# Soft-capped attention into a slot mixture: scores issued right behind tanh, side work in fixed slots, loads per tensor, filler matmuls

## The chip, the cores and the metric

The kernel runs on one NeuronCore of a Trainium2 chip. The core has engines with a queue each that work in order: TensorE (PE in the profile; its weight loads are PEld), VectorE (DVE), ScalarE (ACT), GpSimd (POOL) and SyncE (SP), which here only issues DMAs. TensorE writes to PSUM, eight banks of 2 KB per partition; the other data lie in SBUF. The metric is the device time of one execution in microseconds, the median of several runs. The profile comes from one further execution.

## The reference

Attention over 8 batches x 12 heads, 448 positions, head size 64, with a soft cap on the scores, and behind it a soft mixture of 8 experts with 4 slots each:

```python
scores = scale * q @ k.T                      # per batch and head, scale = 1/8
scores = cap * np.tanh(scores / cap)          # cap = 30
attn = softmax(scores)                        # rows
x = (attn @ v) -> (3584, 768)                 # heads side by side
logits = x @ phi                              # 32 slots
d = softmax(logits, axis=0)                   # over all 3584 rows
slot_input = d.T @ x                          # (8 experts, 4 slots, 768)
slot_out[e] = relu(slot_input[e] @ w1[e]) @ w2[e]     # 768 -> 1024 -> 768
c = softmax(logits, axis=1)                   # over the slots
out = c @ slot_out
```

The attention is where the exponentials are: 8 x 12 x 448 x 448 values go through tanh and then through exp.

## The kernel before, in words

**Tiles.** Four heads of one batch form a quad (24 quads, index Q), two heads a pair (48 pairs). A quad's q, k and v are loaded as f32 (`load`, line 126), 448 KB each, cast to bf16 (`cast`, line 135, on DVE; `vcast`, line 152, on POOL, into block-diagonal tiles `vbd` with a column of ones for the row sums), and q and k are transposed on PE, seven tiles each, with a copy back by DVE (`transp`, line 141). `load` allocates all three raw tiles and issues their three DMAs on SP in the order q, k, v. Each raw tile has one buffer, so a load waits until the cast of the quad before has read it.

**Chunks.** The scores of a pair are seven tiles of 128 keys (two heads of 64) x 448 queries. Four such tiles make a chunk; there are 84 chunks, and seven of them cover two quads. For chunk j: `qk_chunk(j)` (line 166) is eight matmuls into the one PSUM tile `sc` (four banks, one buffer), `tanh_chunk(j)` (line 178) reads it on ACT into `ex`, `exp_chunk(j)` (line 183) works on `ex` in place, and `pv_tile` (line 186), four matmuls per tile, accumulates attention times v and the row sums in `pv`. A pair's seven tiles accumulate in the same two banks, so every seventh tile is a pair's last: there DVE computes reciprocals and scales the result into `xq` (lines 205 and 206), which frees the banks for the next pair. Such a pair's turn falls inside a chunk in three chunks of seven.

**Side work.** Per pair `x_transp` (line 214) transposes `xq`; per quad `logits` (line 223); per batch, that is every three quads, `e_exp` (a small exponential on ACT), `slot_sums` in three parts, `e_transp`, and per two batches `e_sums`. The transposes, the logits and the slot sums share two PSUM buffers (pool `psT`). The expert weights are loaded by POOL's DMA queue, 40 loads spread over the loop: `w1b` (8 tiles), the first 28 blocks of `w2b` into SBUF, the other 36 converted to bf16 in DRAM (`w2d`).

**Order.** The order of each engine's queue is written out by hand; nothing is reordered. The dictionary `aux` maps a chunk number to its side work. One round of the loop (line 333) issues: tanh of j, all 16 matmuls of pv of chunk j-1, all side work of j, the scores of j+1, the exponential of j. On PE the scores of j+1 therefore stand behind everything else of the round. Before the loop come the loads, the clearing of `vbd` on POOL, casts, transposes and `qk_chunk(0)`.

**After the loop.** The last chunk's pv, then the remaining transposes, logits, e_exp and slot sums; then `w2d` is loaded back into SBUF (line 358, on SP, as the attention's SBUF comes free); `layer1` (line 369; PSUM tile `hp`, two buffers), `h_transp`, `layer2` (line 397), and the output stage (from line 425): 28 tiles, each two matmuls, a scaling by ACT or DVE, and a DMA of 384 KB.

Of the kernel before, what the change touches and what calls it, by code (L numbers as in the profile page):

```python
# [8 lines left out]
F32 = mybir.dt.float32  # L9
BF16 = mybir.dt.bfloat16  # L10
# [4 lines left out]
P = 128  # L15
HP = 64
NT = 7
DH = 64
S = 448
CH = 4  # L20
# [7 lines left out]
def kernel(  # L28
# [55 lines left out]
    w1b = [wts.tile([P, NJ, F], BF16, name=f"w1b{e}", tag="w1", bufs=E) for e in range(E)]  # L84
# [13 lines left out]
    wjobs = []  # L98
    for e in range(E):
        for jh in range(NJ // 2):  # L100
            wjobs.append((w1b[e][:, 2 * jh:2 * jh + 2, :],
                          w1r[:, e, 2 * jh:2 * jh + 2, :]))
    for n0 in range(0, R2, 4):
        wjobs.append((w2b[:, n0:n0 + 4, :], w2_src(n0, 4)))
# [3 lines left out]
    for n0 in range(R2, len(blocks), 4):  # L108
        t = dram.tile([P, 4, D], BF16, name=f"w2d{n0}")
        wjobs.append((t, w2_src(n0, 4)))  # L110
        w2d.append(t)
# [14 lines left out]
    def load(Q):  # L126
        b, hq = divmod(Q, NQB)
        for nm, src in (("q", q), ("k", k), ("v", v)):
            t = ld.tile([P, 2, S], F32, name=nm + "raw", tag=nm + "raw")
            sp.dma_start(out=t, in_=bass.AP(  # L130
                tensor=src.tensor, offset=(b * H + 4 * hq) * S * DH,
                ap=[[NT * DH, P], [2 * S * DH, 2], [1, NT * DH]]))
            raws[nm, Q] = t

    def cast(nm, Q):
        t = cst.tile([P, NT, P], BF16, name=nm + "bf", tag=nm + "bf")
        dve.tensor_copy(t.rearrange("p c (h d) -> p h c d", h=2),  # L137
                        raws.pop((nm, Q)).rearrange("p h (c d) -> p h c d", d=DH))
        casts[nm, Q] = t

# [11 lines left out]
    def vcast(Q):  # L152
        raw = raws.pop(("v", Q)).rearrange("p h (c d) -> p h c d", d=DH)
        t = vbds[Q % 2]
        pool.tensor_copy(t[0:HP, :, :, 0:DH], raw[0:HP])  # L155
        pool.tensor_copy(t[HP:P, :, :, DH + 1:VW - 1], raw[HP:P])  # L156

    def init_vbd():
        for t in vbds:
            pool.memset(t, 0.0)  # L160
            pool.memset(t[0:HP, :, :, DH:DH + 1], 1.0)
            pool.memset(t[HP:P, :, :, VW - 1:VW], 1.0)
# [20 lines left out]
    def exp_chunk(j):  # L183
        act.activation(exs[j], exs[j], ACT.Exp, scale=cap)  # L184
# [98 lines left out]

    aux = {}

    def at(j, f, *a):
        aux.setdefault(max(j, 0), []).append((f, a))

    def first_chunk(Q):
        return Q * 2 * NT // CH  # L290

    for Q in range(1, NQ):
        j0 = first_chunk(Q)
        at(j0 - 4, cast, "k", Q)
        at(j0 - 4, cast, "q", Q)
        at(j0 - 3, transp, "k", Q)
        at(j0 - 3, vcast, Q)
        if Q + 1 < NQ:
            at(j0 - 3, load, Q + 1)
        at(j0 - 2, transp, "q", Q)  # L300
    for pr in range(NPAIR):
        jc = (pr * NT + NT - 1) // CH + 1
        Q, h = divmod(pr, 2)
        b, hq = divmod(Q, NQB)
        at(jc + 1, x_transp, pr)
        if h == 1:
            at(jc + 2, logits, Q)
            if hq == NQB - 1:
                at(jc + 3, e_exp, b)
                for part in range(3):  # L310
                    at(jc + 4 + part, slot_sums, b, part, 3)
                if b < B - 1:
                    at(jc + 6, e_transp, b)
                if b % 2 and b < B - 1:
                    at(jc + 7, e_sums, b // 2)
    nw = len(wjobs)
    for n, job in enumerate(wjobs):
        j = 2 + n * (NCH - 8) // nw
        at(j, lambda o, i: pool.dma_start(out=o, in_=i), *job)  # L319


    load(0)
    pool.dma_start(out=phib, in_=moe_phi.rearrange("(jt ji) s -> ji jt s", ji=P))
    init_vbd()
    dve.memset(hpad, 0.0)
    cast("q", 0)
    cast("k", 0)
    vcast(0)
    load(1)
    transp("q", 0)  # L330
    transp("k", 0)
    qk_chunk(0)
    for j in range(NCH):
        tanh_chunk(j)
        if j > 0:
            for t in range((j - 1) * CH, j * CH):
                pv_tile(t)
        for f, a in aux.pop(j, []):
            f(*a)
        if j + 1 < NCH:  # L340
            qk_chunk(j + 1)
        exp_chunk(j)
    for t in range((NCH - 1) * CH, NCH * CH):
        pv_tile(t)
    for j in sorted(aux):
        for f, a in aux[j]:
            f(*a)
# [130 lines left out]
```

## Time and profile before

| | us |
|---|---|
| median of 3 runs | 374.16 (371.19 to 374.2) |
| the profiled execution | 371.95 |
| its span, first to last instruction | 369.8 |
| ACT busy in the span | 294.8 |
| PE busy in the span | 277.5 |
| DVE busy in the span | 159.5 |
| mean granted TensorE clock | 0.881 of full |

Times in the rows of the trace count from the span's start. A row of the timeline has start, duration, engine, line, operation, tiles (out<-in), shapes and count; in brackets stand the idle time of the engine before it and what ended it. A row of the waits has the waiting engine and line, whom it waited for, the total in us, how often, and the longest. In the page's profile by slices (40 equal ones) each digit is a tenth. Matmuls are pipelined, so a group of n takes less than n times one; durations of groups overlap a little with their neighbours.

### The profile page before, as it was taken

Reading aid. Unit: us, or ns where it says so; the run is one execution under the profiler, and the core shown is the slowest. Engines: PE = TensorE matmul, PEld = TensorE weight load, DVE = VectorE, ACT = ScalarE, POOL = GpSimd, SP = SyncE. Lnnn points to the kernel's source line nnn. Section 1 sums busy time; section 2 is a strip of 40 time slices with the busy share of each in tenths; the row PEclk is TensorE's granted clock in tenths of the full one; section 3 lists DMA queues with packets and bytes.
Section 4 is the critical chain, followed back from the end, with each engine's and each line's share of the span. In section 5 each row is a group of like instructions: output and inputs, shape, how many; then the busy total and the mean of one; then the engine's idle time right before and its main releaser. Section 6 shows DMA issues by size and latency. Waiting matters only on the chain.

```text
span 369.8 us, 7691 instructions
## 1 busy us (share of the span) xinstructions
PE 277.5 (75%) x3316; PEld 185.5 (50%) x3316; DVE 159.5 (43%) x403; ACT 294.8 (80%) x194; POOL 83.3 (23%) x113
## 2 busy tenths in 40 slices
PE   2887888779777697888778697777687976697580
PEld 1455655547555465555555464555454654444220
DVE  5234435444454444454364444443643432314552
ACT  1789989997998979999889989999899899013441
POOL 8401331223033214312330340233213200000000
PEclk9999869996899979988898969999989698589956
DMA  8795769873976788698749899899898920682997
GB/s 209 227 230 114 200 177 220 188 197 116 222 203 185 180 163 219 160 248 173 195 138 224 210 249 245 187 281 240 200 190 229 209 86 2 235 364 108 396 398 293
DMA packets 40705, 76.83 MB, mean 208 GB/s; under 512 B 3168, under 2 KB 29792, under 8 KB 40672
## 3 DMA queue, kind: packets, MB, share of 16 engines
q1 hardware_dynamic: 24912, 51.13, 40.4%
q0 software_dynamic: 15760, 25.22, 37.6%
q8 instruction: 26, 0.43, 0.5%
q14 instruction: 7, 0.06, 0.0%
HBM read 90.54 MB, written 18.09 MB: 294 GB/s over the span
## 4 chain that ended last, share of the span: by engine, by line
PE 38%; ACT 37%; DVE 14%; DMA 5%; issue 3%; SPq 0%; DVEq 0%; ACTq 0%
ACT ex L184 19%; ACT ex L181 17%; PE pv L196 14%; PE sc L175 12%; DVE xq L206 7%; DMA out_dram<-ob 3%; PE kps L145 2%; DVE rec L205 2%; DMA kraw<-in_k_dram 2%; PE hp L375 2%; PE xps L218 2%; PE so_ps L401 1%; PE op L433 1%; PE lps L228 1%; DVE ob L437 1%
## 5 line engine op out<-in xcount | busy, mean ns | idle before, releaser
L181 ACT ACTIVATE ex<-sc 128x1792 bf16<-128x1792 f32 x84 | 139.3, 1658 | 31.3 <-PE sc L175 31.1
L196 PE MATMUL pv<-vbd,ex 128*128 128x130 bf16 x1344 | 119.5, 242 | 52.6 <-DVE xq L206 25.4
L184 ACT ACTIVATE ex<-ex 128x1792 bf16<-128x1792 bf16 x84 | 142.5, 1696 | 2.4
L196 PEld LDWEIGHTS <-ex 128*128 128x128 bf16 x1344 | 90.3, 108 | 104.2 <-ACT ex L184 54.5
L175 PE MATMUL sc<-qT,kT 64*64 64x448 bf16 x672 | 81.9, 407 | 2.9 <-ACT ex L181 0.7
L155 POOL CAST vbd<-vraw 64x896 bf16<-64x896 f32 x24 | 22.2, 927 | 208.8 <-PE pv L196 204.5
L205 DVE RECIPROCAL rec<-pv 128x4 f32<-128x4 f32 x96 | 17.0, 177 | 75.1 <-PE pv L196 75.1
L206 DVE TENSOR_TENSOR xq<-pv,rec 128x256 bf16<-128x256 f32 x96 | 40.7, 424 | 3.3
L175 PEld LDWEIGHTS <-kT 64*64 64x64 bf16 x672 | 29.7, 115 | 22.3 <-issue 8.0
L147 DVE COPY qT<-qps 128x896 bf16<-128x896 bf16 x24 | 15.0, 624 | 43.5 <-PE qps L145 43.5
L220 DVE COPY xT<-xps 128x512 bf16<-128x512 bf16 x48 | 20.1, 420 | 21.2 <-PE xps L218 21.2
L218 PE MATMUL xps<-ident,xq 128*128 128x128 bf16 x192 | 21.6, 242 | 8.4 <-DVE qT L147 3.7
L156 POOL CAST vbd<-vraw 64x896 bf16<-64x896 f32 x24 | 22.9, 954 | 1.3
L439 ACT ACTIVATE ob<-op,winv 128x768 f32<-128x768 f32 x14 | 12.5, 901 | 12.6 <-DMA out_dram<-ob 6.9
L433 PE MATMUL op<-so,ET 128*128 128x384 bf16 x56 | 16.4, 394 | 7.0 <-DVE ob L437 4.9
L147 DVE COPY kT<-kps 128x896 bf16<-128x896 bf16 x24 | 14.9, 619 | 13.7 <-PE kps L145 13.7
L218 PEld LDWEIGHTS <-xq 128*128 128x128 bf16 x192 | 15.5, 110 | 10.1 <-issue 9.4
L145 PE MATMUL kps<-ident,kbf 128*128 128x128 bf16 x168 | 17.0, 256 | 3.1 <-DVE kbf L137 3.1
L437 DVE TENSOR_SCALAR ob<-op,winv 128x768 f32<-128x768 f32 x14 | 14.2, 1017 | 10.9 <-DMA out_dram<-ob 5.8
L145 PE MATMUL qps<-ident,qbf 128*128 128x128 bf16 x168 | 14.5, 231 | 5.1 <-DVE qbf L137 5.1
L137 DVE CAST kbf<-kraw 128x896 bf16<-128x896 f32 x24 | 16.0, 666 | 3.4 <-DMA kraw<-in_k_dram 3.4
L319 POOL DMA_DIRECT2D w1b<-in_moe_w_dram x24 | 16.9, 708 | 0.0
(56 smaller groups left out, 157.7 us busy)
## 6 DMA issues: line engine op xcount, KB each, us to landing
w1b<-in_moe_w_dram POOLq DMA_DIRECT2D x24, 512.0 KB, 6.3
qraw<-in_q_dram SPq DMA_DIRECT2D x24, 448.0 KB, 3.9
kraw<-in_k_dram SPq DMA_DIRECT2D x24, 448.0 KB, 4.6
vraw<-in_v_dram SPq DMA_DIRECT2D x24, 448.0 KB, 3.6
out_dram<-ob SPq DMA_DIRECT2D x28, 384.0 KB, 4.5
w2d<-in_moe_w_dram POOLq DMA_DIRECT2D x9, 768.0 KB, 9.2
w2t<-w2d SPq DMA_DIRECT2D x9, 768.0 KB, 7.5
w2b<-in_moe_w_dram POOLq DMA_DIRECT2D x7, 768.0 KB, 8.6
```

The lines of the kernel that those rows point to most:

```text
L145: pe.transpose(ps[:, c, :], src[:, c, :], ident)
L147: dve.tensor_copy(t, ps)
L155: pool.tensor_copy(t[0:HP, :, :, 0:DH], raw[0:HP])
L156: pool.tensor_copy(t[HP:P, :, :, DH + 1:VW - 1], raw[HP:P])
L175: pe.matmul(sc[cs, u, 0:S], qkT["k", Q][r, c, cs], qkT["q", Q][r, :, cs], start=True, stop=True)
L181: act.activation(ex, scores.pop(j)[:, :, 0:S], ACT.Tanh, scale=qk_scale / cap)
L184: act.activation(exs[j], exs[j], ACT.Exp, scale=cap)
L196: pe.matmul(pvs[pr][g // 2][:, g % 2, :], exs[j][:, u, GOFF[g]:GOFF[g] + P], vbds[Q % 2][:, h, c, :], start=(c == 0 and g % 2 == 0), stop= ...
L205: dve.reciprocal(rec, pv[:, :, :, DH:DH + 1])
L206: dve.tensor_tensor(xq[Q][:, 2 * s:2 * s + 2, h * P:(h + 1) * P] .rearrange("p g (i d) -> p g i d", i=2), pv[:, :, :, 0:DH], rec.to_broadc ...
L218: pe.transpose(ps[:, g, :], xq[Q][:, g, h * P:(h + 1) * P], ident)
L220: dve.tensor_copy(t, ps)
```

## The change

Seven things, all in the order of work and in where it lies; the arithmetic of the result is the same.

1. **Loop order.** Each chunk's side work has a slot, "a" or "b". A round issues tanh of j, pv of chunk j-1 up to the pair's turn if one falls inside the chunk (else all of it), slot "a", the scores of j+1, the rest of pv, slot "b", the exponential of j.
2. **Fixed slots.** Side work is placed by a table with a period of seven chunks (`quad_in`, `quad_out`); slot sums come in two parts instead of three, the last ones in one.
3. **Loads per tensor.** Each tensor of a quad is loaded when its own cast has been issued: q and k behind their casts, v behind `vcast`.
4. **First loads.** q and k of quad 0 come as two halves (two heads each), q's on SP and k's on ACT's queue; `first_half` casts, transposes and copies one half, and the scores of chunk 0 stand between the halves. Quad 1 is loaded into a tile `raw1` that lies in a buffer of the w1 weights; the eighth w1 tile is allocated later for that.
5. **Clearing.** `ones` and `vbd` are set by DVE instead of POOL; `hpad` is cleared after the first transposes, phi is loaded later.
6. **Filler matmuls.** `busy(n)` issues n matmuls of `ones` with `ones` into an unused score tile: 30 at the start, 8, 6, 4, 8 and 12 between the steps after the loop. `x_transp` of the last pair but one stands before the last chunk's pv.
7. **Layer 1.** `hp` has three PSUM buffers instead of two.

```diff
-    ones = consts.tile([P, P], BF16, name="ones")
-    pool.memset(ones, 1.0)
+    ones = consts.tile([P, P], BF16, name="ones")
+    dve.memset(ones, 1.0)
...
-    w1b = [wts.tile([P, NJ, F], BF16, name=f"w1b{e}", tag="w1", bufs=E) for e in range(E)]
+    w1b = [wts.tile([P, NJ, F], BF16, name=f"w1b{e}", tag="w1", bufs=E)
+           for e in range(E - 1)]
...
+    def load_w1(e, jh):
+        if e == len(w1b):
+            w1b.append(wts.tile([P, NJ, F], BF16, name=f"w1b{e}", tag="w1", bufs=E))
+        pool.dma_start(out=w1b[e][:, 2 * jh:2 * jh + 2, :],
+                       in_=w1r[:, e, 2 * jh:2 * jh + 2, :])
...
-    def load(Q):
-        b, hq = divmod(Q, NQB)
-        for nm, src in (("q", q), ("k", k), ("v", v)):
+    def load(nm, Q):
+        if Q < NQ:
             t = ld.tile([P, 2, S], F32, name=nm + "raw", tag=nm + "raw")
+            sp.dma_start(out=t, in_=quad_ap(nm, Q))
             raws[nm, Q] = t
+
+    def load_first():
+        for nm in "qkv":
+            raws[nm, 0] = ld.tile([P, 2, S], F32, name=nm + "raw", tag=nm + "raw")
+        for h in range(2):
+            sp.dma_start(out=raws["q", 0][:, h, :], in_=quad_ap("q", 0, h))
+            act.dma_start(out=raws["k", 0][:, h, :], in_=quad_ap("k", 0, h))
+        sp.dma_start(out=raws["v", 0], in_=quad_ap("v", 0))
+        t = wts.tile([P, 3, 2, S], F32, name="raw1", tag="w1", bufs=E)
+        for n, nm in enumerate("kqv"):
+            raws[nm, 1] = t[:, n, :, :]
+            sp.dma_start(out=raws[nm, 1], in_=quad_ap(nm, 1))
+
+    def first_half(h):
+        for nm in ("q", "k"):
+            if h == 0:
+                casts[nm, 0] = cst.tile([P, NT, P], BF16, name=nm + "bf", tag=nm + "bf")
+                qkT[nm, 0] = qk.tile([P, NT, P], BF16, name=nm + "T", tag=nm + "T")
+            dve.tensor_copy(
+                casts[nm, 0][:, :, h * HP:(h + 1) * HP],
+                raws[nm, 0][:, h, :].rearrange("p (c d) -> p c d", d=DH))
+        for nm in ("q", "k"):
+            ps = psT.tile([P, NT, P], BF16, name=nm + "ps", tag="T")
+            r = slice(h * HP, h * HP + HP)
+            for c in range(NT):
+                pe.transpose(ps[r, c, :], casts[nm, 0][:, c, r], ident)
+            dve.tensor_copy(qkT[nm, 0][r], ps[r])
+            if h == 1:
+                raws.pop((nm, 0)), casts.pop((nm, 0))
+                load(nm, 2)
...
         casts[nm, Q] = t
+        if Q > 1:
+            load(nm, Q + 1)
...
+        if Q != 1:
+            load("v", max(Q + 1, 2))
...
     def init_vbd():
         for t in vbds:
-            pool.memset(t, 0.0)
+            dve.memset(t, 0.0)
...
+    PER = 2 * 2 * NT // CH
+    def quad_in(Q, cast_k, cast_q, k_in, q_in):
+        if 0 < Q < NQ:
+            at(*cast_k, cast, "k", Q)
+            at(*cast_q, cast, "q", Q)
+            at(*k_in, transp, "k", Q)
+            at(*k_in, vcast, Q)
+            at(*q_in, transp, "q", Q)
...
+    for m in range(NCH // PER):
+        j = m * PER
+        quad_in(2 * m + 1, (j - 1, "b"), (j, "a"), (j, "b"), (j + 1, "b"))
+        quad_in(2 * m + 2, (j + 3, "b"), (j + 4, "a"), (j + 4, "a"), (j + 5, "b"))
+        if m:
+            at(j, "a", x_transp, 4 * m - 2)
+            at(j + 1, "a", x_transp, 4 * m - 1)
+            quad_out(2 * m - 1, (j + 2, "a"), (j + 3, "a"), ((j + 4, "b"), (j + 6, "a")),
+                     (j + 9, "b"), (j + 10, "b"))
+        at(j + 3, "a", x_transp, 4 * m)
+        at(j + 5, "a", x_transp, 4 * m + 1)
+        quad_out(2 * m, (j + 6, "a"), (j + 7, "a"), ((j + 9, "b"), (j + 10, "b")),
+                 (j + 11, "b"), (j + 13, "a"))
...
+    load_first()
+    junk = psS.tile([P, CH, 512], F32, name="junk", tag="sc")
+
+    def busy(n):
+        for _ in range(n):
+            pe.matmul(junk[:, 0, 0:P], ones, ones, start=True, stop=True)
+
+    busy(30)
+    init_vbd()
+    first_half(0)
+    qk_chunk(0)
+    first_half(1)
+    vcast(0)
+    dve.memset(hpad, 0.0)
     pool.dma_start(out=phib, in_=moe_phi.rearrange("(jt ji) s -> ji jt s", ji=P))
...
     for j in range(NCH):
         tanh_chunk(j)
-        if j > 0:
-            for t in range((j - 1) * CH, j * CH):
-                pv_tile(t)
-        for f, a in aux.pop(j, []):
-            f(*a)
+        ready = list(range((j - 1) * CH, j * CH)) if j else []
+        turn = next((n for n, t in enumerate(ready) if n and t % NT == 0), len(ready))
+        for t in ready[:turn]:
+            pv_tile(t)
+        run(j, "a")
         if j + 1 < NCH:
             qk_chunk(j + 1)
+        for t in ready[turn:]:
+            pv_tile(t)
+        run(j, "b")
         exp_chunk(j)
+    x_transp(NPAIR - 2)
+    junk = psS.tile([P, CH, 512], F32, name="junk", tag="sc")
+    busy(8)
     for t in range((NCH - 1) * CH, NCH * CH):
         pv_tile(t)
-    for j in sorted(aux):
-        for f, a in aux[j]:
-            f(*a)
+    busy(6)
+    x_transp(NPAIR - 1)
+    busy(4)
+    logits(NQ - 1)
+    e_exp(B - 1)
+    busy(8)
+    slot_sums(B - 1, 0, 1)
+    busy(12)
...
-        hp = big.tile([P, 512], F32, name="hp", tag="hp", bufs=2)
+        hp = big.tile([P, 512], F32, name="hp", tag="hp", bufs=3)
```

More of the change, by code (lines that the diff above doesn't have):

```diff
@@ L284, with at @@
     aux = {}
[L286 to L303, printed above, removed]
-        b, hq = divmod(Q, NQB)
[L305 to L315, printed above, removed]
+    def at(j, slot, f, *a):
+        if j < 0:
+            j, slot = 0, "a"
+        aux.setdefault((j, slot), []).append((f, a))
@@ L316, with run @@
     nw = len(wjobs)
     for n, job in enumerate(wjobs):
-        j = 2 + n * (NCH - 8) // nw
-        at(j, lambda o, i: pool.dma_start(out=o, in_=i), *job)
-    load(0)
-    pool.dma_start(out=phib, in_=moe_phi.rearrange("(jt ji) s -> ji jt s", ji=P))
[L324 to L332, printed above, removed]
+        at(2 + n * (NCH - 8) // nw, "b", *job)
+    def run(j, slot):
+        for f, a in aux.pop((j, slot), []):
+            f(*a)
```

41 lines of the change are left out of this document (28 added, 13 removed).

## The prediction, made before the result was known

> **What bounds the kernel now.** I read the page first (shares by engine, granted clock), then the waits, the stages, and single chunks in the timeline.
>
> ```profile
> span 369.8 us, 7691 instructions
> ...
> PE 277.5 (75%) x3316; PEld 185.5 (50%) x3316; DVE 159.5 (43%) x403; ACT 294.8 (80%) x194; POOL 83.3 (23%) x113
> ...
> PEclk9999869996899979988898969999989698589956
> ...
> L181 ACT ACTIVATE ex<-sc 128x1792 bf16<-128x1792 f32 x84 | 139.3, 1658 | 31.3 <-PE sc L175 31.1
> ```
> ```profile
> ACT ex L181 <- PE sc L175: 31.1, 40, 8.9
> ```
> ```profile
> 10.90:314.84 303.94, 238.79 (x2927) 166.79 (x2927) 133.92 (x366) 279.08 (x175) 74.67 (x93) 0.90 0.79 191
> 322.11:330.70 8.59, 7.91 (x104) 3.42 (x108) 0.92 (x2) 1.19 (x2) 0.00 (x0) 0.78 1.02 418
> 337.16:369.80 32.64, 16.65 (x67) 6.19 (x66) 15.01 (x18) 12.49 (x14) 0.00 (x0) 0.75 0.86 338
> ```
>
> The stage rows give length, busy time of PE, PEld, DVE, ACT and POOL, granted clock, DMA share and GB/s. ACT is the busiest engine, and what holds it up is named once: in 40 of 84 chunks tanh waits for its scores, 31.1 us in all. One of these waits (8.9) is the start; 22 us lie in the loop. The loop runs from the first tanh (10.90) to the last exponential's end (314.84).
>
> What a chunk costs undisturbed, and what a pair's turn does to it:
>
> ```profile
> 308.19 1.65 ACT L181 ACTIVATE ex<-sc 128x1792 bf16<-128x1792 f32 x1
> 308.33 1.08 PE L196 MATMUL pv<-vbd,ex 128*128 128x130 bf16 x16 [0.32 <-ACT ex L184]
> 309.25 0.39 PE L218 MATMUL xps<-ident,xq 128*128 128x128 bf16 x4
> 309.86 1.70 ACT L184 ACTIVATE ex<-ex 128x1792 bf16<-128x1792 bf16 x1
> 309.88 0.94 PE L175 MATMUL sc<-qT,kT 64*64 64x448 bf16 x8 [0.24 <-ACT ex L181]
> 311.47 1.65 ACT L181 ACTIVATE ex<-sc 128x1792 bf16<-128x1792 f32 x1
> ```
> ```profile
> 283.42 0.55 PE L145 MATMUL qps<-ident,qbf 128*128 128x128 bf16 x7
> ...
> 285.91 1.65 ACT L181 ACTIVATE ex<-sc 128x1792 bf16<-128x1792 f32 x1
> 286.06 0.40 PE L196 MATMUL pv<-vbd,ex 128*128 128x130 bf16 x4 [0.79 <-ACT ex L184]
> 287.63 0.74 PE L196 MATMUL pv<-vbd,ex 128*128 128x130 bf16 x10 [0.26 <-DVE xq L206]
> 288.21 0.37 PE L228 MATMUL lps<-phib,xT 128*128 128x32 bf16 x8
> 288.51 1.70 PE L175 MATMUL sc<-qT,kT 64*64 64x448 bf16 x8
> 290.14 1.92 PE L196 MATMUL pv<-vbd,ex 128*128 128x130 bf16 x16
> 290.25 1.66 ACT L181 ACTIVATE ex<-sc 128x1792 bf16<-128x1792 f32 x1 [0.97 <-PE sc L175]
> ```
>
> Tanh to tanh is 3.28 us (308.19 to 311.47) when scores come in time: they may start when tanh has read its PSUM tile and must end 1.6 us later; at full clock they take 0.94. In the second fence PE first stands for DVE to empty the finished pair's accumulators, so scores start 1.0 us after tanh's end, at half clock (1.70 instead of 0.94), and ACT waits 0.97. At 3.28 the 84 chunks take 275.5; the loop's excess is 28.4 us. There are two causes in one queue: waits for DVE ahead of the scores, and the clock.
>
> The clock has its own pattern. It changes only on a grid 3.41 us wide; each pair of rows is one stretch and the next:
>
> ```profile
> 223.55:226.96 3.41, 2.18 (x41) 1.38 (x39) 2.16 (x7) 3.38 (x3) 0.00 (x0) 1.00 1.16 210
> 226.97:230.37 3.40, 2.99 (x50) 2.18 (x47) 1.43 (x4) 3.37 (x3) 0.00 (x0) 1.00 1.13 256
> 264.51:267.92 3.41, 2.26 (x40) 1.82 (x36) 1.77 (x6) 2.86 (x2) 1.79 (x2) 1.00 0.79 260
> 267.93:271.33 3.40, 3.26 (x46) 2.29 (x43) 1.38 (x3) 2.96 (x3) 1.45 (x3) 1.00 0.65 144
> 308.88:312.29 3.41, 2.11 (x26) 1.32 (x23) 0.74 (x3) 3.38 (x3) 0.00 (x0) 1.00 0.00 0
> 312.30:315.70 3.40, 2.68 (x28) 2.32 (x29) 1.09 (x4) 2.51 (x2) 0.00 (x0) 0.50 0.00 0
> 213.31:216.71 3.40, 3.40 (x33) 2.26 (x30) 0.56 (x2) 2.43 (x2) 0.00 (x0) 0.50 1.16 210
> 216.72:220.13 3.41, 3.41 (x30) 2.31 (x29) 1.98 (x6) 2.56 (x4) 2.88 (x4) 0.50 0.93 300
> ```
>
> A stretch with PE busy 2.18 or 2.26 keeps full clock in the next; one with 2.11 loses it; a half-clock stretch may be busy throughout (3.40) and still not win it back at once. I take 2.15 us of busy PE as the limit. In the loop the mean is 0.90: with two levels, 1.00 and 0.50, a fifth of its time is at half.
>
> The Trainium skill, page "TensorE: Matmul & The Clock Gate", section "Why this matters for your kernels", asks only that no idle gap of about 3 us stand between bursts of matmuls. The trace is stricter: the stretch from 308.88 lost the clock with 2.11 us of work in 3.41.
>
> **Loop: the scores' new place.** Scores go ahead of the pair-turn remainder, transposes, logits and slot sums. Per seven chunks (call them r0 to r6) three have a turn inside: r2 (after 12 matmuls of pv), r4 (after 8), r6 (after 4). In each, the wait for DVE (about 1.2 us, 286.46 to 287.63) now falls behind the scores, whose own 0.94 us and the rest of tanh cover most of it; what it delays next is the remainder of pv, which has until the exponential's end. Ahead of the scores there remain at most pv x16 and four transposes: 1.08 + 0.39, less their overlap, end at 1.45 after tanh's start (308.19 to 309.64), before tanh's end. At full clock every chunk then takes 3.28: 275.5 us, and I add 0.5 for the seven small exponentials of the slots, an estimate.
>
> The price is a new idle time: PE now waits in order for tanh's end with work queued behind. In r6 it has only 0.40 + 0.37 (logits) before the scores. From r5's scores on, a grid stretch then holds 0.94 (scores) + 0.55 (the transposes of q) + 0.75 = about 2.2, less overlaps of 0.1 to 0.2 = 2.05, under 2.15, if it begins 1.1 to 3.0 us into r5: 1.9 of 3.41 grid positions, 0.56 x 12 periods = 6.7 losses. From r3 (nothing behind its scores) into r4 it holds 0.94 + 0.58 (pv x8) + 0.5 (transposes of k) = 2.0, for 1.2 of 3.41, in the 8 periods without slot sums there: 2.8. That makes 9.5 half-clock stretches in place of about 18 (a fifth of 303.94 is 61 us). Price of one: all at half, pv, x-transposes and scores take 1.92 + 0.6 + 1.70 less 0.2 = 4.0 against 3.28, 0.7 over, if begun on time; nearly nothing if the clock returns before the scores (1.92 + 0.6 + 0.94 less 0.2 = 3.3); 1.8 if r6's 12 late matmuls (1.3 at half) push the next pv. I take 0.6: 5.7 us. Bounds: none at all, 0; as many as now at the 0.97 of the row at 290.25, 17.5.
>
> The first chunks are at half clock too, as their scores' length shows:
>
> ```profile
> 3.95 1.06 DVE L137 CAST qbf<-qraw 128x896 bf16<-128x896 f32 x1 [2.01 <-DMA qraw<-in_q_dram]
> 5.07 0.93 PE L145 MATMUL qps<-ident,qbf 128*128 128x128 bf16 x7 [5.07 <-DVE qbf L137]
> 9.15 1.70 PE L175 MATMUL sc<-qT,kT 64*64 64x448 bf16 x8 [0.72 <-DVE kT L147]
> 10.90 1.66 ACT L181 ACTIVATE ex<-sc 128x1792 bf16<-128x1792 f32 x1 [8.87 <-PE sc L175]
> 22.73 1.66 ACT L181 ACTIVATE ex<-sc 128x1792 bf16<-128x1792 f32 x1 [0.41 <-PE sc L175]
> ```
>
> Three chunks took 11.83 (10.90 to 22.73) against 9.84: 2.0 lost. The fillers may warm the clock, but the wait behind them loses it again; I keep 1.8 (bounds 0 and 2.5). Loop: 275.5 + 0.5 + 5.7 + 1.8 = 283.5, **20.4 saved** (bounds 26.5 and 8).
>
> **Start.** Half loads of q and k go out on two queues, SP's and ACT's; half the channels are cast, transposed and scored first. The whole q landed at 3.95; two halves are as many bytes, so about 3.8. Two half casts (0.3 each, estimate) end at 4.4, but the 30 fillers stand ahead of the transposes: at half clock 0.11 each (1.92 / 16 gives 0.12 with its tail), from about 1.3 to 4.7. Then transposes 0.93, copy 0.6, the second copy 0.6, scores 1.70 or 0.94: first tanh at 8.4, **2.5 saved** (bounds 1.2: the fillers delay, ACT's queue issues late behind its table load; 3.5: warm). The clearing of vbd on DVE lies before 3.8, and if it does not it costs its overhang, under 1. What moves behind (the other half, the clearing of hpad, the next quad's loads) has the first chunk's 3.28 as cover. Loads per tensor wait for their own cast only; each has some 9 us to land, against the time shown here, so nothing; the cover is gone above 9:
>
> ```profile
> DMA to landing us min/median/max: 4.1/4.6/7.0
> ```
>
> Behind a load's wait on SP stand only later loads; vcast on POOL is issued when its buffer's last pv is just done, so the weight loads behind it there gain rather than lose.
>
> **Tail.**
>
> ```profile
> 314.90 1.91 PE L196 MATMUL pv<-vbd,ex 128*128 128x130 bf16 x16 [0.23 <-ACT ex L184]
> 322.11 4.65 PE L375 MATMUL hp<-w1b,slT 128*32 128x512 bf16 x48 [1.26 <-DVE slT L365]
> 327.44 1.48 PE L375 MATMUL hp<-w1b,slT 128*32 128x512 bf16 x24 [0.68 <-ACT hb L379]
> ```
> ```profile
> SPq L358 <- PE pv L196: 20.1, 1, 20.1
> ```
>
> At full clock pv saves 0.8 (1.91 to 1.08) and layer 1 1.7 (4.65 to 2 x 1.48). The transposes moved ahead of the last pv save about 0.4, the third hp bank the wait of 0.68. The 38 fillers lie in waits for DVE and ACT (1.26 before layer 1) and cost nothing there; at half clock 38 x 0.11 = 4.2 us no longer fits everywhere, +0.5. All good: -3.5; cold: -0.5. Late next are the seven w2t loads released by the last pv: 7 x 768 KB at the 418 GB/s of the second stage row are 13 us, which leaves layer 2 some 2 us of room. The output stage (32.64, at its DMA rate) does not change. I take **1.8 saved** (bounds 3.5, and 0.5 lost).
>
> **Sum.** The profiled execution took 371.95, its span 369.8 and 2.15 around it; the median of the runs, 374.16, is 2.2 above it. 371.95 - 20.4 - 2.5 - 1.8 = 347.25, given as 347.5.
>
> **Rivals.**
> 1. The clock never falls in the loop. By the Trainium skill's rule above this would follow, since no idle time comes near 3 us. By rows: loop 275.5 + 0.5 + 1.8 = 277.8, 26.1 saved, 341.5 in all. For it: the new loop has more even work; against it: the row from 308.88.
> 2. The clock falls as often as now, because PE waits for tanh with work behind it: 275.5 + 0.5 + 1.8 + 17.5 = 295.3, 8.6 saved; 371.95 - 8.6 - 4.3 = 359. For it: the 2.05 above, so close to the limit. In its weak form this is the change not doing what it says: the stall changes its name from DVE to the clock.
> 3. Slower: the loop stays at half clock because the transposes, now spread through every chunk, do not count as work. Then each chunk is PE's: pv 1.92, scores 1.70, transposes 44 per period, so 6.3 x 0.11 = 0.7, less 0.3 = 4.0; 0.77 over in each. It passes the kernel before when the loop's loss eats the whole gain, 24.7 + 5.7 = 30.4, at 40 of 84 chunks; all 84 would give 341.5 + 65 = 406. The row from 264.51 speaks against it: 2.26 us busy with 11 transposes among its matmuls (some 0.9 us of it), so under 1.5 without them, and the clock stayed. The Trainium skill, on the same page, section "Part 4: PE-mode transpose", says transposes do not count as busy in the same way; by that rule this is the outcome, and the trace does not agree.
> 4. Loads late: each quad would have to wait over 1 us, landing above 10 us against at most 7.0.
>
> **How the numbers follow.** Forecast 0.68 (341.5 to 353 by itself), rival 1 0.12, rival 2 0.14, rivals 3 and 4 with anything slower 0.06. The range goes from rival 1 to just short of rival 2's value: 341 to 358. A measurement tells some 1% from no change: faster 0.92, same 0.03, slower 0.05.
>
> **What would show it.** Waits of pv for DVE gone from in front of the scores; tanh's wait for scores some 14 us in all (6.4 at the start), the loop's in chunks next to half-clock stretches; granted clock about 0.95 in the loop; first tanh near 8.4; layer 1 begun under 7 us after the last exponential. It would be wrong if the losses stand in r2, r4 or r6 at full clock (then the remainder is late, not the clock), or if DVE waits for raw loads.

## The result and the profile after

| | before | after |
|---|---|---|
| median of 4 runs each, us | 372.68 (369.86 to 374.2) | 341.66 (338.91 to 344.06) |
| ratio, without the run of 344.06 | | 0.9151 (95%: 0.9047 to 0.9256) |
| the profiled execution, us | 371.95 | 338.91 |
| first tanh | 10.90 | 7.51 |
| loop, first tanh to the last exponential's end | 303.94 | 277.21 |
| from there to the span's end | 54.97 | 52.42 |
| time at half clock in the loop, from the first rise on record | 60.6 | 17.1 |

The first row has one run of the kernel before more than the 374.16 above. Ratios here and below are to the kernel before on the same chip and leave out slow runs, those over 1.5% above the fastest of their kernel, here the one of 344.06. The records of the clock begin with its first rise, at 25.58 before and 4.77 after; the first chunks before are at half clock too and are not in the 60.6.

The predicted 347.5 (341 to 358) is 5.8 above the median. The profiled execution after is the fastest of its four runs, 2.75 us under their median; the others took 340.51, 342.82 and 344.06 at mean granted clocks of 0.929, 0.927 and 0.914, against its 0.942. Profile against profile the change saves 33.0, median against median 31.0.

The page of the changed kernel: span, busy time by engine, granted clock in tenths by slice, the chain that ended last, and the two ACT groups of the loop with PE's scores.

```profile
span 337.1 us, 7890 instructions
...
PE 254.3 (75%) x3398; PEld 180.5 (54%) x3398; DVE 160.9 (48%) x414; ACT 289.7 (86%) x194; POOL 88.2 (26%) x106
...
PEclk9699979999999999999999999997999899999755
...
ACT 75%; PE 7%; DMA 6%; DVE 3%; SPq 3%; issue 3%; DVEq 0%; ACTq 0%
...
L230 ACT ACTIVATE ex<-sc 128x1792 bf16<-128x1792 f32 x84 | 138.3, 1647 | 5.4 <-PE sc L224 5.4
...
L224 PE MATMUL sc<-qT,kT 64*64 64x448 bf16 x672 | 72.7, 364 | 31.1 <-ACT ex L230 25.5
```

ACT's own work is the same (142.5 us of exponentials in both, 138.3 of tanh against 139.3); what went is its wait for scores (31.1, now 5.4, of which the first chunk's start is 4.6), and the wait has changed sides: PE now stands for tanh, 25.5 us, where that costs nothing but the clock now and then. The waits say it once more (engine and line, whom it waited for, total, times, longest):

```profile
POOL vbd L202 <- DMA vraw<-in_v_dram: 20.6, 3, 8.4
...
ACT ex L230 <- PE sc L224: 5.4, 4, 4.6
```

The stages of the changed kernel (length; busy time of PE, PEld, DVE, ACT, POOL; granted clock; DMA share; GB/s): the loop, the last exponential to layer 1, layers 1 and 2, the output.

```profile
7.51:284.72 277.21, 214.83 (x2953) 159.28 (x2952) 135.31 (x371) 273.95 (x175) 86.52 (x96) 0.97 0.88 210
284.72:291.07 6.35, 4.56 (x86) 3.79 (x86) 2.94 (x9) 0.31 (x1) 0.00 (x0) 1.00 0.64 216
291.07:304.32 13.25, 12.08 (x240) 6.68 (x241) 1.83 (x4) 1.31 (x3) 0.00 (x0) 1.00 0.79 316
304.32:337.10 32.78, 17.36 (x68) 6.29 (x67) 15.38 (x18) 12.84 (x15) 0.00 (x0) 0.67 0.86 336
```

Of the 32.7 us that the span lost, 26.7 left the loop, 3.4 the start and 2.55 the end. The loop is now 84 x 3.28 = 275.5 and 1.7 more. A pair's turn (r6) and the chunk behind it, in the timeline, at a place where the clock also fell:

```profile
258.05 1.65 ACT L230 ACTIVATE ex<-sc 128x1792 bf16<-128x1792 f32 x1
...
258.19 0.40 PE L245 MATMUL pv<-vbd,ex 128*128 128x130 bf16 x4 [0.29 <-ACT ex L233]
...
259.29 0.42 DVE L255 TENSOR_TENSOR xq<-pv,rec 128x256 bf16<-128x256 f32 x1
...
259.74 0.94 PE L224 MATMUL sc<-qT,kT 64*64 64x448 bf16 x8 [0.95 <-DVE xq L255]
...
260.62 3.11 PE L245 MATMUL pv<-vbd,ex 128*128 128x130 bf16 x28
261.33 1.65 ACT L230 ACTIVATE ex<-sc 128x1792 bf16<-128x1792 f32 x1
...
264.08 0.78 PE L224 MATMUL sc<-qT,kT 64*64 64x448 bf16 x8
...
264.93 1.66 ACT L230 ACTIVATE ex<-sc 128x1792 bf16<-128x1792 f32 x1 [0.17 <-PE sc L224]
```

DVE empties the accumulators until 259.71, but the scores do not stand behind that: they start at 259.74 because tanh (258.05 + 1.65) has just ended (the bracket names the later releaser by 0.01), and the next tanh comes 3.28 after the last one, at 261.33. The 12 late matmuls and the 16 of the next chunk then run as one row of 28, at half clock in its first part, and the chunk takes 3.60 instead of 3.28. That is the price of the lost clock here: 0.3.

### The profile page after: what moved, and what is told of

Read it like the earlier page. It is cut to its first block, busy times and chain, and to the rows that moved or that the text cites. A ratio compares the mean times of both kernels' runs of the same rounds, so it can differ in the third digit from the quotient of the medians.

```text
span 337.1 us, 7890 instructions
## 1 busy us (share of the span) xinstructions
PE 254.3 (75%) x3398; PEld 180.5 (54%) x3398; DVE 160.9 (48%) x414; ACT 289.7 (86%) x194; POOL 88.2 (26%) x106
## 4 chain that ended last, share of the span: by engine, by line
ACT 75%; PE 7%; DMA 6%; DVE 3%; SPq 3%; issue 3%; DVEq 0%; ACTq 0%
ACT ex L233 38%; ACT ex L230 37%; DMA w2t<-w2d 4%; SPq L521 3%; PE pv L245 2%; PE sc L224 2%; DMA out_dram<-ob 1%; DMA qraw<-in_q_dram 1%; PE op L514 1%; DVE ob L518 1%; DVE xq L255 1%; ACT E L288 0%; PE slps L321 0%; DVE kT L175 0%; PE qps L174 0%
## 5 line engine op out<-in xcount | busy, mean ns | idle before, releaser
L233 ACT ACTIVATE ex<-ex 128x1792 bf16<-128x1792 bf16 x84 | 142.5, 1696 | 2.4
L230 ACT ACTIVATE ex<-sc 128x1792 bf16<-128x1792 f32 x84 | 138.3, 1647 | 5.4 <-PE sc L224 5.4
L245 PE MATMUL pv<-vbd,ex 128*128 128x130 bf16 x1344 | 101.7, 227 | 27.8 <-ACT ex L233 26.9
L245 PEld LDWEIGHTS <-ex 128*128 128x128 bf16 x1344 | 81.3, 101 | 54.3 <-ACT ex L233 39.5
L224 PE MATMUL sc<-qT,kT 64*64 64x448 bf16 x672 | 72.7, 364 | 31.1 <-ACT ex L230 25.5
L202 POOL CAST vbd<-vraw 64x896 bf16<-64x896 f32 x23 | 21.6, 939 | 175.3 <-PE pv L245 154.7
L224 PEld LDWEIGHTS <-kT 64*64 64x64 bf16 x672 | 35.3, 106 | 43.9 <-issue 27.9
L203 POOL CAST vbd<-vraw 64x896 bf16<-64x896 f32 x23 | 30.9, 1344 | 1.3
L514 PE MATMUL op<-so,ET 128*128 128x384 bf16 x56 | 17.1, 406 | 5.3 <-DVE ob L518 3.5
L267 PE MATMUL xps<-ident,xq 128*128 128x128 bf16 x192 | 19.0, 221 | 0.6 <-DVE xq L255 0.6
L514 PEld LDWEIGHTS <-ET 128*128 128x128 bf16 x56 | 6.0, 109 | 15.4 <-issue 14.2
L182 DVE CAST qbf<-qraw 128x896 bf16<-128x896 f32 x22 | 14.0, 636 | 0.0
L192 PEld LDWEIGHTS <-qbf 128*128 128x128 bf16 x161 | 9.3, 99 | 8.6 <-issue 8.2
L192 PE MATMUL kps<-ident,kbf 128*128 128x128 bf16 x161 | 12.9, 220 | 1.2 <-DVE kbf L182 0.9
```

Of the source, the lines that this page charges most:

```text
L192: pe.transpose(ps[:, c, :], src[:, c, :], ident)
L224: pe.matmul(sc[cs, u, 0:S], qkT["k", Q][r, c, cs], qkT["q", Q][r, :, cs], start=True, stop=True)
L230: act.activation(ex, scores.pop(j)[:, :, 0:S], ACT.Tanh, scale=qk_scale / cap)
L245: pe.matmul(pvs[pr][g // 2][:, g % 2, :], exs[j][:, u, GOFF[g]:GOFF[g] + P], vbds[Q % 2][:, h, c, :], start=(c == 0 and g % 2 == 0), stop= ...
L267: pe.transpose(ps[:, g, :], xq[Q][:, g, h * P:(h + 1) * P], ident)
L514: pe.matmul(op[:, half, 0:HD], et_tile(bb, c), so[half], start=True, stop=True)
```

## The experiments

Unless said otherwise each is the changed kernel with one edit. "Loop" and "first tanh" are read from its profile as above. Each profile is one run, and the changed loop, or one that differs from it only in its loads, took 276.94 to 281.74 in the profiles below, so a difference of under 5 us between two loops can be chance.

**Only the order of the loop, in the kernel before.** All side work keeps its old list and goes behind the scores.

```diff
-        if j > 0:
-            for t in range((j - 1) * CH, j * CH):
-                pv_tile(t)
+        ready = list(range((j - 1) * CH, j * CH)) if j else []
+        turn = next((n for n, t in enumerate(ready) if n and t % NT == 0), len(ready))
+        for t in ready[:turn]:
+            pv_tile(t)
+        if j + 1 < NCH:
+            qk_chunk(j + 1)
+        for t in ready[turn:]:
+            pv_tile(t)
         for f, a in aux.pop(j, []):
             f(*a)
-        if j + 1 < NCH:
-            qk_chunk(j + 1)
```

> The kernel before with the loop order alone changed: pv up to the turn, scores, the rest of pv, then all side work of that chunk at its old place in the list; loads, start and tail are the old ones. Theory A: the order alone brings the loop from 303.9 to 277 to 284, the time to 345 to 353. Rival (the fixed slots matter as much, because side work bunched behind the scores pushes the next pv past the half-clock limit or past tanh): loop 290 or more, time 358 or more.

Measured: 347.11 (344.7 to 350.65), 0.9427 (0.9336 to 0.9518) of the kernel before; loop 282.01. The order alone saves 21.9 of the loop's 26.7, and this profile is of the slowest of its four runs. What the other 4.8 were stands in its timeline: three times (chunks 7, 21 and 63) a turn at half clock throws the next chunk back.

```profile
33.04 1.70 PE L175 MATMUL sc<-qT,kT 64*64 64x448 bf16 x8 [1.15 <-ACT ex L181]
34.67 1.48 PE L196 MATMUL pv<-vbd,ex 128*128 128x130 bf16 x12
34.78 1.66 ACT L181 ACTIVATE ex<-sc 128x1792 bf16<-128x1792 f32 x1
35.95 0.42 PE L228 MATMUL lps<-phib,xT 128*128 128x32 bf16 x8
36.21 1.89 PE L196 MATMUL pv<-vbd,ex 128*128 128x130 bf16 x16
...
38.03 1.33 PE L175 MATMUL sc<-qT,kT 64*64 64x448 bf16 x8
...
39.42 1.66 ACT L181 ACTIVATE ex<-sc 128x1792 bf16<-128x1792 f32 x1 [1.25 <-PE sc L175]
```

Scores 1.70, 12 late matmuls 1.48, logits, then pv 1.89 and scores again: 4.64 from tanh to tanh, 1.36 lost. This is the dear case of the prediction's clock price (there 1.8). It need not be a loss by the old slots: the changed loop meets such a case too, twice in each of two profiles below. Outside its loop this run spent 68.6 us (350.65 less 282.01); if the fastest run, of 344.7, spent as much, its loop took about 276, an estimate, and the order alone then brings all of the 26.7.

**Scores behind everything, all else as changed.**

```diff
         run(j, "a")
-        if j + 1 < NCH:
-            qk_chunk(j + 1)
         for t in ready[turn:]:
             pv_tile(t)
         run(j, "b")
+        if j + 1 < NCH:
+            qk_chunk(j + 1)
```

> The changed kernel with one part undone: the scores of the next chunk stand behind all of pv and both slots again; slots, loads, fillers and tail stay. Theory A (the place of the scores carries the loop's gain): tanh waits for scores in most chunks again, over 20 us in the loop, the loop (first tanh to last exponential) 298 to 306 us against 277.2, the time 362 to 372. Theory B (the loop gains from the clock, which evener side work and fillers hold up, wherever the scores stand): loop under 285, granted clock above 0.92, time under 350.

Measured: 355.89 (355.1 to 359.13), 0.9705 (0.9616 to 0.9794); loop 293.11. Neither expectation holds. The scores' place is worth 15.9 us of loop; but even with the scores last, the slots, the loads and the start are worth 303.94 - 293.11 = 10.8. So the two parts overlap: order first, 21.9 + 4.8, of which the 4.8 can be chance; slots first, 10.8 + 15.9. Of the 17.6 us over 3.28 per chunk, 7.3 lie in r4, 6.6 of them in three chunks behind one wait that the prediction had not seen:

```profile
76.16 0.61 POOL L293 COPY e<-E 128x512 bf16<-128x512 bf16 x1
...
76.83 0.61 PE L297 MATMUL eps<-ident,e 128*128 128x128 bf16 x4 [1.50 <-POOL e L293]
77.37 1.33 PE L224 MATMUL sc<-qT,kT 64*64 64x448 bf16 x8
...
78.75 1.66 ACT L230 ACTIVATE ex<-sc 128x1792 bf16<-128x1792 f32 x1 [2.52 <-PE sc L224]
```

PE stands for POOL's copy of e with the scores behind it. In the changed kernel the same wait, there 0.97, lies behind the scores and tanh does not wait for it.

**No split at the turn.** All 16 matmuls of pv go ahead of the scores; the rest of the side work stays.

```diff
-        turn = next((n for n, t in enumerate(ready) if n and t % NT == 0), len(ready))
+        turn = len(ready)
```

> The changed kernel with the whole of pv ahead of the scores, also where a pair turns inside the chunk; slot b stays behind the scores. If the wait of pv for DVE at a turn is what delayed the scores, the three chunks of seven with a turn (12, 8 and 4 matmuls before it) lose about 0.3, 0.6 and 0.4 us each: 12 x 1.3 = 16 us more in the loop, less at half clock less even: loop 290 to 297, time 354 to 361. If the side work between pv and scores was the delay and the turn's wait lies under tanh anyway: loop 277 to 280, time as the changed kernel's (339 to 344).

Measured: 351.9 (347.68 to 360.8), 0.9541 (0.9427 to 0.9656); loop 290.51, tanh's waits:

```profile
ACT ex L230 <- PE sc L224: 16.4, 26, 4.7
```

The loop lies in the range of the first expectation, the time 2 us under it. The split alone is worth 13.3 us of loop. The turn in r2, with 12 matmuls ahead of it, lost nothing (0.3 each was expected); over 3.28 per chunk the losses lie in r4 (5.3), r5 (1.8) and r6 (6.4).

**No filler matmuls** (`range(n)` in `busy` becomes `range(0)`).

> The changed kernel without any filler matmul; they contribute to no result. If the fillers hold the clock: scores of chunk 0 take 1.70 instead of 0.94 and the transposes 0.93, first tanh at 8.3 to 8.8 instead of 7.5, the first four chunks lose about 2 us instead of 0.5, the last pv, slot sums and the first layer-1 matmuls run at half clock and layer 1 begins 7 us after the last exponential instead of 6.4: in all 3 to 5 us slower. If the fillers only fill waits and the clock is set by the other work: within 1 us of the changed kernel, first tanh 7.0 to 7.5.

Measured: 345.97 (342.13 to 346.37), 0.9395 (0.9304 to 0.9486); first tanh 8.98, loop 278.76, last exponential to layer 1 6.52. The start against that of the changed kernel, first here, then there:

```profile
4.83 0.95 PE L174 MATMUL qps<-ident,qbf 128*64 128x128 bf16 x7 [4.83 <-DVE qbf L167]
...
7.24 1.70 PE L224 MATMUL sc<-qT,kT 64*64 64x448 bf16 x8 [0.71 <-DVE kT L175]
...
8.98 1.66 ACT L230 ACTIVATE ex<-sc 128x1792 bf16<-128x1792 f32 x1 [6.04 <-PE sc L224]
```
```profile
1.06 3.38 PE L392 MATMUL junk<-ones 128*128 128x128 bf16 x30 [1.06 <-DVE ones L67]
...
4.68 0.60 PE L174 MATMUL qps<-ident,qbf 128*64 128x128 bf16 x7 [0.24 <-DVE qbf L167]
...
6.52 0.94 PE L224 MATMUL sc<-qT,kT 64*64 64x448 bf16 x8 [0.74 <-DVE kT L175]
...
7.51 1.66 ACT L230 ACTIVATE ex<-sc 128x1792 bf16<-128x1792 f32 x1 [4.57 <-PE sc L224]
```

Without fillers transposes and scores run at half clock: 1.5 us of first tanh, and 1.1 more in the first four chunks. Profile against profile the kernel is 3.2 slower, as the first expectation has it. After the loop the fillers are worth 0.2: without them layer 1 takes 5.37 instead of 4.07, but layer 2 then has no wait for its last load.

**First q and k whole, both from SP's queue.**

```diff
-        for h in range(2):
-            sp.dma_start(out=raws["q", 0][:, h, :], in_=quad_ap("q", 0, h))
-            act.dma_start(out=raws["k", 0][:, h, :], in_=quad_ap("k", 0, h))
+        sp.dma_start(out=raws["q", 0], in_=quad_ap("q", 0))
+        sp.dma_start(out=raws["k", 0], in_=quad_ap("k", 0))
```

> The changed kernel with q and k of the first quad loaded whole, both from SP; casts and transposes by halves as in the change. If the halves on two queues carry the start: the first cast waits until about 4.0 for q as before and k comes at 5.2 to 5.7, first tanh at 8.6 to 9.2 instead of 7.6, 1 to 1.5 us slower. If the start is carried by the warm clock and the halved copies: first tanh at 7.6 to 8.0.

Measured: 344.33 (343.15 to 345.52), 0.9378 (0.9254 to 0.9501); first tanh 8.19, between the two expectations: q's cast starts at 4.03 (4.01 changed), k's at 5.24 (4.54). Halves on two queues are worth 0.7, through k alone. The loop, 280.77, is 3.6 longer than the changed one although nothing in it differs; two chunks (14 and 56, both r0) carry 3.1 of it, like this one:

```profile
53.20 1.70 PE L223 MATMUL sc<-qT,kT 64*64 64x448 bf16 x8 [0.95 <-DVE xq L254]
...
54.83 3.22 PE L244 MATMUL pv<-vbd,ex 128*128 128x130 bf16 x28
54.94 1.66 ACT L229 ACTIVATE ex<-sc 128x1792 bf16<-128x1792 f32 x1
...
58.40 1.33 PE L223 MATMUL sc<-qT,kT 64*64 64x448 bf16 x8
...
59.79 1.66 ACT L229 ACTIVATE ex<-sc 128x1792 bf16<-128x1792 f32 x1 [1.41 <-PE sc L223]
```

Here the clock fell at 53.15, just ahead of r6's scores, and for two stretches; in the changed kernel's profile it fell at 260.77, 1.03 behind their start, and for one. The first costs 1.57 (54.94 to 59.79 against 3.28), the second 0.32. Where the 3.41 grid lies against the chunks is an accident of the execution.

**Loads of the next quad together, behind `vcast`** (the two `load` lines of `cast` and `vcast` become one loop over q, k, v in `vcast`).

> The changed kernel with the three loads of the next quad issued together again, q, k, v behind vcast. The prediction costed loads per tensor at nothing. If that holds: loop 276.5 to 278, no wait of DVE for raw q or k in the loop, time within 2 us of the changed kernel (338 to 342). If the earlier issue matters, k of the quad after next is needed 7.5 us after its issue in every second quad and 10 us in the others, against 5 to 7 us to land with the weights on the way: waits for k of 1 to 2 us in every second quad, most of them under PE's slack, loop 280 or more.

Measured: 343.32 (338.42 to 344.79), 0.9277 (0.8912 to 0.9642): wide enough for any answer. Its loop took 281.74, with the same two dear chunks as above and a cold start. DVE waited for a raw k twice in the loop, 0.20 at 103.37 and 1.09 at 266.89, as the second expectation has it but far more seldom, and no tanh waited behind either. So by the waits loads per tensor are worth nothing for the loop; by the time it is not decided.

**Two banks for hp instead of three.**

> The changed kernel with two PSUM buffers for hp. If layer 2 is bound by the w2t loads at its end: layer 1 waits 0.7 for the bank again, layer 2 starts 0.7 later, its own wait for the last w2t shrinks from 1.2 to 0.5, the end of layer 2 stays 19.2 to 19.6 after the last exponential, the time within 0.5 of the changed kernel. If not bound: 0.7 later, 20.0 or more.

Measured: 341.82 (340.25 to 343.76), 0.9327 (0.9162 to 0.9491). Layers 1 and 2 take 13.25, to the hundredth what they take with three; the wait for the last w2t load is 0.3 instead of 1.17, and layer 2 ends 19.6 after the last exponential in both. The third bank is hidden behind that load, as expected.

**The changed kernel again, and one that holds the clock.** The holding kernel puts 8 matmuls of `ones` with `ones` into slot b of r3 and slot a of r6, the thin places named in the prediction, where no slot sums lie.

```diff
+    def hold(n):
+        ps = psT.tile([P, P], F32, name="hold", tag="T")
+        for _ in range(n):
+            pe.matmul(ps, ones, ones, start=True, stop=True)
...
+        if m not in (2, 5, 8, 11):
+            at(m * PER + 3, "b", hold, 8)
+        if m not in (3, 6, 9):
+            at(m * PER + 6, "a", hold, 8)
```

> The changed kernel itself once more, beside the next three on the same chip: 339 to 344, loop 277 to 282, three to eight half-clock stretches in the loop, at other places than in the first profile, since the grid of the clock does not start with the kernel.

> The changed kernel with eight more fillers per period in the two thin places of the loop: behind the scores in r3 and ahead of them in r6 (not in the periods where slot sums lie there). They contribute to no result. If the half-clock stretches in the loop come from too little matmul work in a stretch of the grid: none is left after the first chunks, the loop is 276.0 to 276.9, the time 1 to 3 us under the changed kernel's median. If they come from something else, or the fillers push the scores: as many as in the changed kernel, loop 277.2 or more.

Measured on one chip, six runs each: changed again 339.53 (338.4 to 345.22), 0.9192 (0.9136 to 0.9248); holding 338.96 (338.29 to 339.49), 0.9167 (0.9123 to 0.9212). The medians are the same within their intervals, but the spread falls from 4.0 us (6.8 with the longest run) to 1.2, and all six mean clocks lie between 0.954 and 0.959 (0.927 to 0.949 without). The accident of the grid has little left to act on. The first expectations were not met in full. The changed loop, 276.94, lost the clock behind its start at two places, 46.08 and 261.12, almost those of the first profile. The holding loop took 277.53, no less: its first four chunks happened to lose 1.09 instead of 0.47, and one half-clock stretch was left behind them, at 277.30, in a period whose r3 has no fillers. In all 10.2 us of it are at half clock.

**The same fillers as transposes** (`pe.transpose(ps, ones, ident)`), one run.

> The same fillers at the same places, as transposes instead of matmuls (same 128 columns, nothing reads them). If transposes count as work for the clock: no half-clock stretch in the loop after the first chunks, as with matmuls. If they do not count (the Trainium skill's section on the transpose): half-clock stretches remain, two to eight of them, at r3 to r4 and r5 to r6.

Measured: 339.71, loop 277.51, 10.2 us of it at half clock, as with matmuls. A thin stretch from r5 to r6, here (first row; the second is the stretch behind it) and in the changed kernel:

```profile
188.63:192.04 3.41, 2.62 (x38) 1.83 (x37) 2.43 (x7) 3.38 (x3) 0.00 (x0) 1.00 1.11 272
192.05:195.45 3.40, 3.16 (x48) 2.50 (x47) 1.52 (x5) 3.40 (x4) 1.40 (x2) 1.00 1.16 211
```
```profile
257.35:260.76 3.41, 2.16 (x32) 1.52 (x31) 2.44 (x7) 3.38 (x3) 0.00 (x0) 1.00 1.07 254
260.77:264.18 3.41, 3.41 (x36) 3.21 (x36) 0.59 (x3) 3.41 (x4) 0.38 (x1) 0.50 1.15 206
```

With eight filler transposes, 0.61 us of the 2.62, the clock stays; without them, at 2.16, it goes. One pair could be chance, as a stretch of so little work sometimes keeps the clock; but this loop has five such stretches, and by the count of columns worked out below all five would lie under the limit without the filler transposes (2,650 to 2,930). Transposes count as work here.

**Holding, also at the start, and w2t loads early.** Besides `hold`: 16 more fillers around the scores of chunk 1, in a free accumulator bank, and the pools `qk` and `vb` change places, so that three w2t loads need not wait for the last pv.

```diff
-    vb = att.enter_context(tc.tile_pool(name="vb", bufs=1))
     qk = att.enter_context(tc.tile_pool(name="qk", bufs=2))
+    vb = att.enter_context(tc.tile_pool(name="vb", bufs=1))
...
         run(j, "a")
+        if j == 0:
+            fill0(8)
         if j + 1 < NCH:
             qk_chunk(j + 1)
+        if j == 0:
+            fill0(8)
```

> The loop's fillers as matmuls, 16 more around the scores of chunk 1, which hold the clock through the first wait for loads, and the SBUF pools of qk and vb exchanged, so that three w2t loads instead of two lie over tiles that are free before the last pv. Expected: first four chunks lose under 0.3 instead of 0.6; the last w2t no longer stops layer 2 (its wait of 1.17 gone); time 336 to 339, 3 to 5 us under the changed kernel's median. If the tail is not bound by the w2t loads, end of layer 2 stays 19.5 us after the last exponential.

Measured: 337.1 (336.85 to 339.03), 0.9132 (0.9089 to 0.9175), on the chip of the two kernels above and 2.4 under the changed kernel's median there; five of its six runs lie below the changed kernel's fastest. Its loop, layers 1 and 2, and output:

```profile
7.62:283.72 276.10, 218.56 (x3105) 162.64 (x3104) 135.01 (x371) 273.67 (x175) 86.81 (x96) 1.00 0.90 215
290.07:301.97 11.90, 11.90 (x240) 6.68 (x241) 1.83 (x4) 1.31 (x3) 0.00 (x0) 1.00 0.52 210
301.97:335.20 33.23, 16.70 (x67) 6.15 (x67) 15.38 (x18) 12.86 (x15) 0.00 (x0) 0.70 0.85 332
```

Full clock through the whole loop: 276.10 is its floor, 275.5 for the chunks and 0.6 for the small exponentials. PE is busy throughout layers 1 and 2 (11.90 of 11.90), so the w2t wait is gone; the output stage is 0.45 longer, for a reason that stays open.

## Why the prediction was right, and which step was off

| term, profile against profile | predicted | measured |
|---|---|---|
| start (first tanh) | -2.5 | -3.39 |
| loop | -20.4 | -26.73 |
| end | -1.8 | -2.55 |
| sum | -24.7 | -32.7 |

The loop saved 0.2 more than the bound of 26.5 set for it; the prediction's own terms, without the clock's losses and the cold chunks, give 303.94 - 276.0 = 27.9, so the bound was drawn too tight.

**The loop's cause: right.** The scores left the queue behind DVE and the chunks run at 3.28. In the changed profile no chunk at full clock loses more than the small exponential's 0.05, in r2, r4 or r6 either; taking the split or the order away brings back 13.3 and 15.9. That the new slots alone would bring 10.8 with the scores last was not foreseen. It did not matter for the sum, since order and slots remove in part the same waits.

**The clock's term: place right, size wrong.** The prediction said that stretches from r5 (1.1 to 3.0 into it) and from r3 (1.2 to 2.4) would lose the clock. In the changed profile three stretches of the loop lost it behind the start: from 42.31 (1.41 into r3), 226.63 (1.73 into r3) and 257.35 (2.59 into r5). So the places held. But there were 3, not 9.5: two from r3 for the 2.8 of the forecast, one from r5 for 6.7. Six stretches began in r5's interval; the other five held 2.47 to 3.12 us of work, two of them with slot sums, two where the transposes of e had pushed r5's work into them, one behind a half-clock stretch with pv still to do. The count had left these out. And each loss cost 0 to 0.32, not 0.6, since they all fell where the late matmuls had room. The term was 5.7 + 1.8 for the first chunks; in the profile it is 0.6 + 0.6. This is the step that failed: 6.3 of the 8 us by which the sum was off, for the fastest run. The median run was 2.75 slower, and part of the term may come back there: the dear case (1.36 to 1.57 each) was met in three other kernels' profiles, two of them with the changed loop. No profile of that run shows it.

**The clock's limit: the wrong measure.** The prediction took 2.15 us of busy PE in a stretch as the limit. These are two stretches of the changed kernel, each with the one behind it:

```profile
158.37:161.78 3.41, 2.04 (x28) 1.35 (x27) 1.77 (x6) 3.38 (x3) 1.65 (x2) 1.00 0.79 197
161.79:165.19 3.40, 3.04 (x50) 2.40 (x49) 0.83 (x2) 3.37 (x3) 1.39 (x2) 1.00 0.65 210
226.63:230.04 3.41, 2.04 (x27) 1.43 (x28) 1.76 (x6) 3.38 (x4) 0.93 (x1) 1.00 1.16 215
230.05:233.45 3.40, 3.40 (x39) 2.53 (x36) 1.14 (x3) 3.37 (x3) 2.06 (x2) 0.50 1.10 286
```

Both are busy for 2.04 us; the first keeps the clock, the second loses it. What parts them is the columns: 130 for a matmul of pv, 128 for a transpose, what the rows give for the others, and for one of the scores a quarter of its 448, since its tile is 64*64 and not 128*128 (the quarter is a fit, 112 columns). The first holds about 9.1 of pv, 7 transposes and 8.9 of the scores, 3,080 columns; the second 8, 7 and 8.7, 2,910. Counted so, one limit of some 3,030 columns tells in the first 280 us of all thirteen profiles whether the next stretch has full clock, from full clock and from half alike, with 2 errors in 1,067 stretches. No limit in busy time has fewer than 70; without the transposes in the count none has fewer than 60. That the chip counts in this way is not shown, only that the count fits. It also accounts for busy half-clock stretches that win nothing: at half rate they hold too few columns (the one from 11.60 in the changed kernel, busy throughout, holds about 2,980).

**The rivals.** Rival 1, a clock that never falls, gave 341.5, close to the median, but for another reason than the trace shows: the clock does fall, mostly where that costs little. That the median fell inside the range is in part luck: it lies 0.7 above the lower end, which rival 1 set, and the profiled run (338.91) and the later median (339.53) lie below that end. The stretch from 257.35 lost the clock with no idle time of PE longer than 0.95. So the rule of the Trainium skill (page "TensorE: Matmul & The Clock Gate", section "Why this matters for your kernels"), to leave no idle gap above about 3 us between bursts of matmuls, is not enough here. With fillers the case comes true, at 337.1. Rival 2, as much half clock as before, did not come: 17.1 us instead of 60.6 in the loop, and 31.6 with the order alone. Rival 3, transposes that do not count, is excluded by the filler transposes and by the count of columns. The Trainium skill, same page, section "Part 4: PE-mode transpose", says that transposes do not count as busy in the same way; these runs do not agree. Rival 4: DVE never waited for q or k in the loop. The loads of v did land later than the prediction allowed, up to 10.1 us after their issue, and POOL waited for them three times, 20.6 us in all, once at the start (5.1 before 6.88) and twice in the loop (7.2 before 55.95, 8.4 before 102.53); but no pv waited for POOL's casts.

**The start: mechanism right, one term too careful.** The prediction took the fillers as too late to warm the clock. They warmed it by 4.77, just ahead of the transposes: 0.60 and 0.94 instead of 0.93 and 1.70. The measured 3.39 is near its warm bound, 3.5. k's halves on ACT's queue carry 0.7 of it, the fillers 1.5; no run takes the other 1.2 apart. The warm start is likely, not sure: in one of ten profiles with these fillers the first tanh came only at 8.88.

**The end: mechanism right, size short by 0.75.** Layer 1 runs as one row of 72 at full clock, 4.07 instead of 4.65 for 48; and "late next" came as named:

```profile
291.07 4.07 PE L456 MATMUL hp<-w1b,slT 128*32 128x512 bf16 x72 [0.58 <-DVE slT L446]
...
299.87 2.77 PE L482 MATMUL so_ps<-w2t,hpad 128*32 128x384 bf16 x64
303.81 0.51 PE L482 MATMUL so_ps<-w2t,hpad 128*32 128x384 bf16 x8 [1.17 <-DMA w2t<-w2d]
```

Layer 2 waits 1.17 for the last w2t load, which takes back what the third hp bank gives; two banks cost nothing. Fillers at the end, which the prediction priced at half clock too, cost nothing and gain 0.2.

## What to carry to other kernels

Put work that feeds the bounding engine ahead of anything in its queue that waits for a third engine, and let the waits gather behind it; look then for the waits that this merely hides, since they return when the order changes. When PE is given idle time, add up its columns per clock stretch in the thinnest places: a handful of filler matmuls there buys little in the best run and much in the worst. Judge such a kernel by several runs: one profile shows one position of the grid.

## What the runs showed of the hardware

- The 3.41 us grid of the clock is not tied to the kernel's start: in nine profiles with the same fillers at the start its first rise came anywhere from 4.24 to 5.37 us, in a tenth, where the grid cut the fillers in two (2.45 us of work in the stretch from 0.10 to 3.51), only at 20.58. Loops alike then took 276.94 to 281.74, mainly by which chunks the half-clock stretches met.
- What keeps or wins the clock follows the columns in a stretch (limit about 3,030, fitted above), not PE's busy time: one with 1.90 us kept it (the last kernel, from 14.75), one with 2.38 lost it (two hp banks, from 181.82). Matmuls of ones with ones count, and so do transposes.
- The mean clock does not give the time: one run with whole first loads took 343.15 at a mean clock of 0.949, one with two hp banks 342.45 at 0.966, where the changed kernel, on another chip, took 338.4 at 0.949. These were not the profiled executions; what held them up stays open.
